# Third subtiles of at most 64 tokens in the experts' second product: 64-column fp32 matmuls in pairs instead of 24 split matmuls

## The chip, the cores and the metric

One core of a Trainium2 chip runs the whole program. The metric is the device time of one execution in microseconds (us), as the median of three runs. A profile of a further execution shows what each engine did: PE (TensorE, matmuls; PEld are its weight loads), DVE (VectorE), ACT (ScalarE), POOL (GpSimd) and SP (SyncE, which issues most of the DMAs).

## The reference

Three stages follow each other. Attention over keys and values that are pooled by 8, a mixture of experts, and a dense feed-forward layer:

```
attn = softmax(scale * q @ mean8(k).T) @ mean8(v)          # 8 x 8 heads, 576 tokens, 64 wide
x = tokens of attn                                          # 4608 x 512, fp32
skip tokens with x @ w_skip <= 0; e = argmax(x @ w_gate)    # 8 experts
h = relu(x[e] @ w1[e])                                      # 512 -> 1024
x[e] += gate * (h @ w2[e])                                  # 1024 -> 512
out = (silu(x @ w_in)) @ w_out                              # 512 -> 2048 -> 512
```

Which tokens go to which expert is known only when the program runs, and the change lies in the middle stage alone.

## The kernel before, in words

An expert's tokens are worked through in units of at most 384 tokens, three subtiles of 128. A list of units (`ut`) is made on the chip; one unit runs ahead of a loop, one behind it, and the loop `For_i` in `moe` takes the others, here 10. A unit has one of three widths by its number of tokens n: 384 (n over 320), 320 (n over 256) or 256. An expert with little more than 384 tokens is shared out so that its second unit has 256 tokens and up to 64 in the third subtile.

Each fp32 factor is split into a high part of the type fp32r and a low part that is the rest (`split`: ACT writes the high part, DVE the low one), and a product is made of three matmuls: high by high, low by high, high by low. In a unit:

- `mm1(n)` makes h for eight blocks f of 128 hidden columns. For each f, 12 matmuls of n columns go into one bank (tile `hp`, three banks in turn). Then ACT writes `hh[:, f]` and DVE `hl[:, f]`, and `conv2(raw2, f)` splits the raw w2 of the unit's expert, which lies in `raw2`, into `w2h` (ACT) and `w2l` (DVE).
- `second(e, cols, nxt, n, third)` first issues `load2(e)` (SP: raw w2 of the next unit's expert e into `raw2`, four DMAs, each of which waits until the two blocks it overwrites have been split). Then follow `xtrans((0, 1))` (transposes of the next unit's tokens on PE, split to `xth` and `xtl`), `gates()`, and `mm2(s, gt)` for the subtiles 2 and 1, each in a `tc.If(n > 128 s)`. Behind subtile 2 come its scatter (POOL) and `conv1(0..3)`, which splits the next expert's w1. At the end stand `xtrans((2, 3))` and `mm2(0, gt)`.
- `mm2(s, gt)` is 24 matmuls of 128 stationary columns by 512 (hh by w2h, hh by w2l, hl by w2h, for eight f) into tile `yp`, of which there are two banks, and one DVE instruction that scales by the gate and adds the tokens (`y`, shown as tile `x`).

All instructions of an engine run in the order in which they are written (class `Ordered`), and across the engines semaphores carry the waits. Nearly all rows bear the line L110, the helper that records them, so tiles tell them apart. `nc.before` and `nc.after` keep the instructions around an If in order on every engine.

Of the kernel before, what the change touches and what calls it, by code (L numbers as in the profile page):

```python
# [5 lines left out]
F32 = mybir.dt.float32  # L6
# [6 lines left out]
AF = mybir.ActivationFunctionType  # L13
ALU = mybir.AluOpType
# [4 lines left out]
P = 128  # L19
B, H, S, D = 8, 8, 576, 64  # L20
G = 72
NT = B * S
DM = H * D
# [129 lines left out]
class Kern:  # L153
# [638 lines left out]
    def moe(self, xa, up):  # L792
        nc, tc, c = self.nc, self.tc, self.c
        with tc.tile_pool(name="ms", bufs=1) as s1, \
             tc.tile_pool(name="mw", bufs=2) as s2, \
             tc.tile_pool(name="mp", bufs=2, space=PSUM) as pp:
            raw2, xn, xth, xtl, gi, si = self.raw2, self.xn, self.xth, self.xtl, self.gi, self.si
            hh = s1.tile([P, 8, U * P], F32R, name="hh", tag="hh")
            hl = s1.tile([P, 8, U * P], F32R, name="hl", tag="hl")
            xr = s1.tile([P, U, XW], F32, name="xr", tag="xr")  # L800
            y = self.x4[:, 0:U]

# [4 lines left out]
            def mm1(n, fs=range(8), conv=True):  # L807
                for f in fs:
                    ps = self.hp.tile([P, DM], F32, name=f"hp{f}_{n}", tag="hp")
                    i = 0  # L810
                    for w, x in ((self.w1h, xth), (self.w1h, xtl), (self.w1l, xth)):
                        for k in range(4):
                            nc.tensor.matmul(ps[:, 0:n], w[:, k, P * f:P * (f + 1)], x[:, k, 0:n],
                                             start=(i == 0), stop=(i == 11))
                            i += 1
                    self.split(hh[:, f, 0:n], hl[:, f, 0:n], ps[:, 0:n], relu=True)
                    if conv:
                        self.conv2(raw2, f)
                    else:
                        nc.scalar.copy(self.w2h[:, f], raw2[:, f])  # L820

            def scatter(s, other=None, si=si):

                ids = self.s2 if s == 2 and si is self.si else si[:, s:s + 1]
                ins = nc.gpsimd.indirect_dma_start(xa, bass.IndirectOffsetOnAxis(ap=ids, axis=0), y[:, s],
                                                   None, bounds_check=NT - 1, oob_is_err=False)
                if other:
                    tc.declare_no_dep(ins.ins, other.ins, reason="disjoint rows")
                return ins

            def gates():
                L = xr[:, :, DM:XW]
                v = nc.vector
                mx = s2.tile([P, U], F32, name="gmx", tag="gmx")
                v.tensor_reduce(mx, L, AX.X, ALU.max)
                d = s2.tile([P, U, E], F32, name="gd", tag="gd")
                v.tensor_tensor(d, L, bc(mx, 2, E), ALU.subtract)
                nc.scalar.activation(d, d, AF.Exp)
                gt = s2.tile([P, U], F32, name="gt", tag="gt")
                v.tensor_reduce(gt, d, AX.X, ALU.add)  # L840
                v.tensor_scalar(gt, gt, 1e-9, None, ALU.add)
                v.reciprocal(gt, gt)
                return gt

            def mm2(s, gt, between=None):
                ps = (pp if s else self.hp).tile([P, DM], F32, name=f"yp{s}", tag="yp" if s else "hp")
                i = 0
                for f in range(8):
                    if between and f == 4:
                        between()  # L850
                    for h, w in ((hh, self.w2h), (hh, self.w2l), (hl, self.w2h)):
                        nc.tensor.matmul(ps, h[:, f, P * s:P * (s + 1)], w[:, f], start=(i == 0), stop=(i == 23))
                        i += 1
                nc.vector.scalar_tensor_tensor(y[:, s, 0:DM], ps, gt[:, s:s + 1], xr[:, s, 0:DM], ALU.mult, ALU.add)

            load2 = lambda e: self.load_w2(e, raw2)
            for _ in self.slow:
                pass
            while len(self.todo) > 2:
                self.step()  # L860
            self.step()
            mm1(U * P, (0, 1), False)
            self.cpool = pp, "xt", 2, DM
            for f in range(3):
# [7 lines left out]
            for f, n in ((2, 5), (3, 7), (4, 7), (5, 7)):  # L872
                mm1(U * P, (f,), False)
                for _ in range(n):
                    next(units)
            self.read_table(nc.gpsimd)
            mm1(U * P, (6,), False)

            def low2(f):
# [9 lines left out]
            def second(e, cols, nxt, n=None, third=None):  # L889

                if n is not None:
                    load2(e)
                    self.xtrans((0, 1))
                gt = gates()
                self.rows(gi, nxt)
                nc.vector.tensor_scalar(self.s2, cols[:, U - 1:U] if third is None else third, -1.0, None, ALU.add)

                def convert(f):
                    for _ in self.ffn_ops(f):
                        pass  # L900
                    self.ffn_conv3(f)
                    self.ffn_load(f + 3)

                if n is None:
                    self.ffn_abs(0, self.raw1[:, 0], self.raw1[:, 1])
                    convert(0)
                for s in (2, 1):
                    if n is None:
                        mm2(s, gt)
                    else:  # L910
                        with tc.If(n > P * s) as cmp:
                            nc.before(cmp)
                            mm2(s, gt)
                        nc.after(cmp)
                    if s == 2:
                        scatter(s)
                        nc.vector.tensor_scalar(si[:, 0:U - 1], cols[:, 0:U - 1], -1.0, None, ALU.add)
                        if n is not None:
                            self.conv1(0)
                            self.conv1(1)  # L920
                            self.conv1(2)
                            self.conv1(3)
                if n is None:
                    self.xtrans((0, 1))
                    mm2(0, gt, lambda: self.xtrans((2, 3)))
                else:
                    self.xtrans((2, 3))
                    mm2(0, gt)
# [6 lines left out]
            for f in range(4, 8):  # L935
                low2(f)
            next(units)
            second(None, self.table[:, SLOTS:EMPTY], entry(1, 1, EMPTY, dve))
            for s in (1, 0, 2):
                nc.scalar.copy(y[:, s, DM:XW], xr[:, U - 1, DM:XW])  # L940
# [3 lines left out]
            with tc.For_i(0, nu, 1, iteration_sync="reg_based") as u:  # L944
                ld = lambda i, o, hi: nc.value(self.ut[0:1, i, bass.ds(u + o, 1)], hi)
                e = ld(0, 1, E - 1)
                self.load_w1(e)
                keep()
                n = ld(2, 0, U * P)
                cols, third = [self.table[:, bass.ds(ld(i, 0, EMPTY), m)] for i, m in ((1, U - 1), (3, 1))]  # L950
                nxt = ld(1, 2, EMPTY)
                self.gather(gi)
                scatter(1)
                scatter(0)
                with tc.If(n > 320) as cmp:
                    mm1(384)
                with cmp.Else():
                    with tc.If(n > 256) as cmp2:
                        mm1(320)
                    with cmp2.Else():  # L960
                        mm1(256)
                nc.after(cmp)
                second(e, cols, nxt, n, third)
# [23 lines left out]
            gt = gates()  # L987
# [11 lines left out]
            for s in (2, 1):  # L999
# [3 lines left out]
                while done:  # L1003
                    f = done.pop(0)
# [6 lines left out]
            while done:  # L1011
                f = done.pop(0)
# [554 lines left out]
```

## Time and profile before

| | us |
|---|---|
| median of three runs | 1315.89 (1315.4 to 1318.23) |
| the profiled execution's own time | 1316.77 |
| its span, first to last instruction | 1315.0 |
| PE busy | 1263.7 (96%) |
| DVE, ACT, POOL busy | 853.5, 569.4, 358.6 |
| the loop's four units of width 320 | 32.1, 31.8, 32.5, 33.8 |

The last row is read from the trace between the first `mm1` matmul of a unit and that of the next one. The loop runs from about 214 to 502 us of the span. The granted TensorE clock is at full speed (0.997 in the mean).

### The profile page before, as it was taken

How to read it: one execution, taken by the hardware profiler on the slowest of the kernel's cores; microseconds unless marked ns; L12 is line 12 of the kernel's file. 1: busy time of each engine (PE TensorE's matmuls, PEld its weight loads, DVE VectorE, ACT ScalarE, POOL GpSimd, SP SyncE). 2: the span in 40 equal slices, each digit the busy share in tenths (PEclk: the TensorE clock that was granted, in tenths of full speed). 3: DMA queues.
4: the chain of work that ended last, by engine and by line, in shares of the span. 5: the costliest groups of instructions: out<-in, count | busy, mean ns of one | idle time of the engine just before them, and what ended most of it. 6: DMA issues, size and time to landing. Idle time of an engine off the chain costs nothing.

```text
span 1315.0 us, 20410 instructions
## 1 busy us (share of the span) xinstructions
PE 1263.7 (96%) x6501; PEld 1076.1 (82%) x6502; DVE 853.5 (65%) x1553; ACT 569.4 (43%) x1188; POOL 358.6 (27%) x312
## 2 busy tenths in 40 slices
PE   6899788999989999999999999999999999999998
PEld 5788677988978888878888888788888888888887
DVE  4777776667667677779743325565784657847565
ACT  4666633454445454344433334534353333533321
POOL 4477433222223230322457603101011010111100
PEclk9999999999999999999999999999999999999999
DMA  9988635656556552248845322634356352463532
GB/s 288 294 271 250 211 129 197 202 178 208 181 181 210 196 191 84 89 164 277 280 169 210 141 97 88 224 124 172 120 185 210 142 176 93 163 208 129 176 106 95
DMA packets 94106, 233.77 MB, mean 178 GB/s; under 512 B 15068, under 2 KB 26972, under 8 KB 90375
## 3 DMA queue, kind: packets, MB, share of 16 engines
q1 hardware_dynamic: 86735, 215.82, 49.3%
q0 software_dynamic: 7008, 16.80, 3.9%
q8 instruction: 42, 0.69, 0.2%
q14 instruction: 33, 0.27, 0.1%
q10 hardware_dynamic: 288, 0.20, 0.1%
HBM read 182.58 MB, written 52.89 MB: 179 GB/s over the span
## 4 chain that ended last, share of the span: by engine, by line
PE 57%; DVE 3%; ACT 1%; issue 1%; POOL 0%; DMA 0%; DVEq 0%; ACTq 0%; POOLq 0%
PE yb L110 20%; PE ps L110 17%; PE fh L110 9%; PE fop L110 9%; PE yp L110 1%; DVE fr L110 1%; DVE ft L110 1%; PE hp L110 1%; PE fxp L110 0%; DVE raw L110 0%; PE sx L110 0%; DVE fgl L110 0%; DVE fsg L110 0%; ACT g L110 0%; DMA out<-fo 0%
## 5 line engine op out<-in xcount | busy, mean ns | idle before, releaser
L110 PE MATMUL yb<-wout,g 128*128 128x512 f32 x1152 | 268.5, 391 | 0.8 <-ACT st L110 0.4
L110 PEld LDWEIGHTS yb<-wout,g 128*128 128x128 f32 x1152 | 215.0, 188 | 45.7 <-DMA wout<-wdo 0.8
L110 POOL TENSOR_TENSOR tm<-tm,tm 128x512 f32<-128x512 f32 x24 | 32.1, 1339 | 411.5 <-ACT tm L110 411.5
L110 DVE TENSOR_TENSOR yacc<-yb,yacc 128x512 f32<-128x512 f32 x168 | 116.1, 691 | 38.2 <-PE yb L110 31.1
L110 ACT COPY tm<-ps 128x512 f32<-128x512 f32 x72 | 42.4, 589 | 146.2 <-PE ps L110 144.4
L110 PE MATMUL yp<-w2h,hh 128*128 128x512 f32 x240 | 96.4, 402 | 1.7 <-ACT w2h L110 1.3
L110 PE MATMUL yp<-w2l,hh 128*128 128x512 f32 x240 | 94.3, 393 | 2.2 <-DVE w2l L110 2.2
L110 PE MATMUL yp<-w2h,hl 128*128 128x512 f32 x240 | 94.3, 393 | 0.0
L110 ACT CAST g<-sg 128x512 fp32r<-128x512 f32 x96 | 59.6, 621 | 76.7 <-DVE sg L110 76.7
L110 ACT ACTIVATE hh<-hp 128x256 fp32r<-128x256 f32 (+2 forms) x96 | 41.2, 429 | 118.0 <-PE hp L110 107.0
L110 ACT ACTIVATE prb<-s,mx 128x72 f32<-128x72 f32 x288 | 65.4, 344 | 46.0 <-DVE mx L110 43.7
L110 DVE TENSOR_TENSOR fsg<-fh,fsg 128x512 f32<-128x512 f32 x48 | 33.0, 688 | 80.0 <-ACT fsg L110 80.0
L110 PE MATMUL fh<-w1l,fh 128*128 128x512 f32 x336 | 83.4, 390 | 0.0
L110 DVE TENSOR_TENSOR tm<-ps,tm 128x512 f32<-128x512 f32 x24 | 16.6, 690 | 98.1 <-PE ps L110 98.1
L110 PE MATMUL hp<-xth,w1h 128*128 128x256 f32 (+2 forms) x384 | 71.3, 307 | 5.3 <-issue 2.5
L110 PE MATMUL hp<-xtl,w1h 128*128 128x256 f32 (+2 forms) x384 | 72.2, 306 | 2.3 <-DVE xtl L110 1.9
L110 PEld LDWEIGHTS fh<-w1l,fh 128*128 128x128 f32 x336 | 62.8, 188 | 12.9
L110 DVE SCALAR_TENSOR_TENSOR hl<-hp,hh 128x256 fp32r<-128x256 f32 (+2 forms) x96 | 46.0, 479 | 40.5 <-ACT hh L110 36.6
L110 PE MATMUL hp<-xth,w1l 128*128 128x256 f32 (+2 forms) x384 | 69.9, 304 | 0.0
L110 DVE TENSOR_TENSOR g<-sg,g 128x512 fp32r<-128x512 f32 x96 | 65.7, 686 | 5.5 <-ACT g L110 5.1
L110 DVE TENSOR_TENSOR w2l<-raw,w2h 128x512 fp32r<-128x512 f32 x96 | 65.9, 691 | 3.3
L110 PE MATMUL pv<-vex,pts 120*128 120x148 f32 (+3 forms) x400 | 61.8, 308 | 4.9 <-remote 2.5
(230 smaller groups left out, 2750.2 us busy)
## 6 DMA issues: line engine op xcount, KB each, us to landing
raw<-w SPq DMA_DIRECT2D x88, 512.0 KB, 3.8
wout<-wdo SPq DMA_DIRECT2D x48, 512.0 KB
win<-wdi SPq DMA_DIRECT2D x36, 512.0 KB
w1l<-wdi SPq DMA_DIRECT2D x36, 512.0 KB
xa<-x SPq DMA_DIRECT2D x36, 256.0 KB
fx<-xa SPq DMA_DIRECT2D x9, 1024.0 KB
v<-vR SPq DMA_DIRECT2D x7, 1200.0 KB
fr<-w_in SPq DMA_DIRECT2D x16, 512.0 KB
```

The costliest lines, as they stand in the source:

```text
L110: ins = f(*a, **k)
```

## The change

In a unit of width 320 the third subtile's 64 tokens are no longer split. `mm1` splits the first 256 columns as before, and ACT writes the relu of the last 64 columns as plain fp32 into a new tile `hx`. In `second` the branch for subtile 2 gets a further `tc.If(n > 320)`: a unit with more tokens does `mm2(2)`, the others a new `mm2_half`. This makes eight fp32 matmuls with `hx[:, f]` as 64 stationary columns and the raw w2 block `raw2[:, f]` as 512 moving columns. Even f write the rows 0 to 63 of one bank, odd f the rows 64 to 127. ACT copies the upper half out, DVE adds the lower half to it, and a second DVE instruction scales by the gate and adds the tokens. As `mm2_half` reads `raw2`, the issue of `load2(e)` is moved from the start of `second` to behind the branch for subtile 2, in all units.

```diff
@@ -797,6 +797,7 @@
+            hx = s1.tile([P, 8, D], F32, name="hx", tag="hx")
...
-                    self.split(hh[:, f, 0:n], hl[:, f, 0:n], ps[:, 0:n], relu=True)
+                    if n == 2 * P + D:
+                        self.split(hh[:, f, 0:2 * P], hl[:, f, 0:2 * P], ps[:, 0:2 * P], relu=True)
+                        nc.scalar.activation(hx[:, f], ps[:, 2 * P:n], AF.Relu)
+                    else:
+                        self.split(hh[:, f, 0:n], hl[:, f, 0:n], ps[:, 0:n], relu=True)
...
+            def mm2_half(gt):
+                ps = pp.tile([P, DM], F32, name="yq", tag="yp")
+                for f in range(8):
+                    o = D * (f % 2)
+                    nc.tensor.matmul(ps[o:o + D], hx[:, f], raw2[:, f], start=(f < 2), stop=(f >= 6),
+                                     skip_group_check=True)
+                o = y[0:D, 2, 0:DM]
+                nc.scalar.copy(o, ps[D:P])
+                nc.vector.tensor_tensor(o, ps[0:D], o, ALU.add)
+                nc.vector.scalar_tensor_tensor(o, o, gt[0:D, 2:3], xr[0:D, 2, 0:DM], ALU.mult, ALU.add)
...
             def second(e, cols, nxt, n=None, third=None):
 
                 if n is not None:
-                    load2(e)
                     self.xtrans((0, 1))
...
                         with tc.If(n > P * s) as cmp:
                             nc.before(cmp)
-                            mm2(s, gt)
+                            if s == 2:
+                                with tc.If(n > 2 * P + D) as cmp2:
+                                    mm2(s, gt)
+                                with cmp2.Else():
+                                    mm2_half(gt)
+                            else:
+                                mm2(s, gt)
                         nc.after(cmp)
+                        if s == 2:
+                            load2(e)
```

The change moves instructions on ACT, PE and SP. On ACT, in `mm1` of width 320, this stood for the blocks f = 0 to 2 (the bracket names the engine or DMA queue whose semaphore is waited for; `raw_80` is `raw2`):

```order
L110 ACTIVATE hh<-hp_320_2934 128x320 [waits PE_I-2728_own,Activation_I-2728_own]
L110 REGISTER_ALU
L110 CAST w2h<-raw_80 128x512 [waits DMAHW4_I-2728_own,Activation_I-2728_own]
L110 ISA
L110 ACTIVATE hh<-hp_320_2951 128x320 [waits PE_I-2728_own,Activation_I-2728_own]
L110 REGISTER_ALU
L110 CAST w2h<-raw_80 128x512 [waits Activation_I-2728_own]
```

and now stands, for f = 0 and 1:

```order
L110 ACTIVATE hh<-hp_320_2935 128x256 [waits PE_I-2729_own,Activation_I-2729_own]
L110 REGISTER_ALU
L110 ACTIVATE hx<-hp_320_2935 128x64 [waits DVE_I-2729_own]
L110 REGISTER_ALU
L110 CAST w2h<-raw_80 128x512 [waits DMAHW4_I-2729_own,Activation_I-2729_own]
L110 ISA
L110 ACTIVATE hh<-hp_320_2953 128x256 [waits PE_I-2729_own,Activation_I-2729_own]
L110 REGISTER_ALU
L110 ACTIVATE hx<-hp_320_2953 128x64 [waits DVE_I-2729_own]
```

Between `hh` and `w2h` of each block ACT has a third instruction, and that one waits for DVE: it reads the same bank as DVE's `hl` of the block, and stands behind it.

On PE, the else branch of the inner If holds the eight matmuls of `mm2_half`; here are those for f = 0 to 3:

```order
L110 MATMUL yq<-raw_80,hx 64x512 [waits Activation_I-2729_own,DMAHW4_I-2729_own,DMAHW2_49]
L110 REGISTER_ALU
L110 MATMUL yq<-raw_80,hx 64x512 [waits Activation_I-2729_own]
L110 REGISTER_ALU
L110 MATMUL yq<-raw_80,hx 64x512 [waits DMAHW5_I-2729_own,Activation_I-2729_own,DMAHW3_49]
L110 REGISTER_ALU
L110 MATMUL yq<-raw_80,hx 64x512 [waits Activation_I-2729_own]
```

Lower and upper rows alternate, and every matmul waits for ACT's `hx` of its own block.

On SP, around the branch for subtile 2, `load2` stood ahead of it:

```order
L110 DMA raw_80<-w 128x2x512 [waits DMAHW4_I-2728_own,DVE_I-2728_own]
L110 ISA
L110 DMA raw_80<-w 128x2x512 [waits DMAHW5_I-2728_own,DVE_I-2728_own]
L110 ISA
L110 DMA raw_80<-w 128x2x512 [waits DMAHW6_I-2728_own,DVE_I-2728_own]
L110 ISA
L110 DMA raw_80<-w 128x2x512 [waits DMAHW7_I-2728_own,DVE_I-2728_own]
L911 COMPARE_AND_BRANCH
```

and now stands behind it:

```order
L926 COMPARE_AND_BRANCH [waits DVE_49]
L929 COMPARE_AND_BRANCH
L929 UNCONDITIONAL_BRANCH x2
L926 UNCONDITIONAL_BRANCH
L110 ISA
L110 DMA raw_80<-w 128x2x512 [waits DVE_I-2729_own,DMAHW4_I-2729_own,PE_I-2729_own,Activation_I-2729_own]
L110 ISA
L110 DMA raw_80<-w 128x2x512 [waits DVE_I-2729_own,DMAHW5_I-2729_own,PE_I-2729_own,Activation_I-2729_own]
```

The four DMAs of w2 now wait for PE as well, and no longer start one by one while `mm1` runs.

## Rows read from the trace of the kernel before

**Rows 1.** Page, part 1: busy time of PE, its share, instructions.
```profile
PE 1263.7 (96%) x6501; PEld 1076.1 (82%) x6502; DVE 853.5 (65%) x1553; ACT 569.4 (43%) x1188; POOL 358.6 (27%) x312
```
**Rows 2.** Stretch of one unit: length, busy by engine, clock, DMA share, GB/s.
```profile
332.40:364.19 31.79, 31.79 (x181) 28.86 (x180) 20.20 (x36) 13.94 (x26) 6.74 (x6) 1.00 0.53 177
```
**Rows 3.** Groups by form, 250 to 520 us: count, busy us, mean ns, idle before.
```profile
L110 PE MATMUL hp<-xth,w1h 128*128 128x320 f32 x128 | 24.0, 309 | 0.0
...
L110 ACT ACTIVATE hh<-hp 128x320 fp32r<-128x320 f32 x32 | 14.0, 438 | 44.9 <-PE hp L110 42.5 <-PE xtp L110 2.4
L110 DVE SCALAR_TENSOR_TENSOR hl<-hp,hh 128x256 fp32r<-128x256 f32 x32 | 13.6, 424 | 7.9 <-ACT hh L110 5.7 <-issue 1.2 <-ACT w2h L110 0.6
L110 ACT ACTIVATE hh<-hp 128x256 fp32r<-128x256 f32 x32 | 12.3, 385 | 35.9 <-PE hp L110 34.4 <-PE xtp L110 1.5
```
**Rows 4.** Timeline of PE in this unit: start, us, operation, count.
```profile
332.40 0.75 PE L110 MATMUL hp<-xth,w1h 128*128 128x320 f32 x4
...
346.48 0.82 PE L110 MATMUL xtp<-ident,xn 128*128 128x128 f32 x6
347.05 0.47 PE L110 MATMUL yp<-w2h,hh 128*128 128x512 f32 x1
...
358.07 0.82 PE L110 MATMUL xtp<-ident,xn 128*128 128x128 f32 x6
...
364.19 0.64 PE L110 MATMUL hp<-xth,w1h 128*128 128x256 f32 x4
```
**Rows 5.** Timeline of PE in attention: fp32 scores, 64 and 128 stationary columns.
```profile
44.37 1.25 PE L110 MATMUL s<-kbd,q 128*64 128x144 f32 x16
...
47.55 1.14 PE L110 MATMUL s<-kbd,q 128*128 128x144 f32 x8
```
**Rows 6.** The scores by tile: duration of one record, least, median, most (ns).
```profile
L110 PE MATMUL s<-kbd,q x320: 283/286/609, 9.4 to 158.9; 128*128 128x144 f32 x128, 128*64 128x144 f32 x32
```
**Rows 7.** Timeline of PE in attention: probabilities by values, 64 stationary columns.
```profile
55.75 2.54 PE L110 MATMUL pv<-vex,pts 120*64 120x148 f32 x20
```
**Rows 8.** Timeline of the weight loads there: idle before, in brackets.
```profile
55.75 2.27 PEld L110 LDWEIGHTS pv<-vex,pts 120*64 120x64 f32 x20 [0.17 <-PE pt L110]
58.22 0.54 PEld L110 LDWEIGHTS s<-kbd,q 128*128 128x128 f32 x4 [0.20 <-PE pv L110]
```
**Rows 9.** Timeline of ACT in the unit of rows 2.
```profile
346.76 0.44 ACT L110 ACTIVATE hh<-hp 128x320 fp32r<-128x320 f32 x1 [0.81 <-PE xtp L110]
347.10 0.61 ACT L110 CAST w2h<-raw 128x512 fp32r<-128x512 f32 x1
...
351.00 0.22 ACT L110 ACTIVATE gd<-gd 128x24 f32<-128x24 f32 x1 [2.54 <-DVE gd L110]
```
**Rows 10.** Timeline of DVE in the unit of rows 2.
```profile
347.23 0.49 DVE L110 SCALAR_TENSOR_TENSOR hl<-hp,hh 128x320 fp32r<-128x320 f32 x1 [0.56 <-ACT hh L110]
347.74 0.69 DVE L110 TENSOR_TENSOR w2l<-raw,w2h 128x512 fp32r<-128x512 f32 x1
...
350.73 0.18 DVE L110 TENSOR_TENSOR gd<-xr,gmx 128x24 f32<-128x24 f32 x1
...
352.12 0.15 DVE L110 TENSOR_SCALAR sq<-table 128x1 int32 x1
...
353.49 0.16 DVE L110 TENSOR_SCALAR si<-table 128x2 int32 x1
353.55 4.62 DVE L110 TENSOR_TENSOR w1l<-raw,w1h 128x1024 fp32r<-128x1024 f32 x4
...
359.19 1.02 DVE L110 TENSOR_TENSOR xtl<-xtp,xth 128x384 fp32r<-128x384 f32 x2 [0.17 <-ACT xth L110]
```
**Rows 11.** Page, part 5: evictions of a whole bank by ACT and DVE.
```profile
L110 ACT COPY tm<-ps 128x512 f32<-128x512 f32 x72 | 42.4, 589 | 146.2 <-PE ps L110 144.4
...
L110 DVE TENSOR_TENSOR tm<-ps,tm 128x512 f32<-128x512 f32 x24 | 16.6, 690 | 98.1 <-PE ps L110 98.1
```
**Rows 12.** A stretch in which raw w1 (2 MB) is loaded; columns of rows 2.
```profile
324.00:332.00 8.00, 8.00 (x40) 6.67 (x39) 4.16 (x6) 1.49 (x3) 0.00 (x0) 1.00 0.76 265
```

## The prediction

> **What bounds the kernel now.** I read the page first: PE is busy for 1263.7 of 1315.0 us [rows 1], so time is gained only where PE gets less to do, or waits less. The change lies in the loop over expert units, so next I cut the span into units by the first `mm1` matmul of each, and looked at the stretch from 332.40 to 364.19 us, a unit of width 320. PE is busy in all of its 31.79 us, at full granted clock, while DVE has 20.20 and ACT 13.94 us of work [rows 2]. Such a unit is bound by PE alone. How many units are touched follows from the form of `mm1`'s matmuls: 128 records of 320 columns in the group of xth and w1h [rows 3], 32 in a unit (8 blocks f by 4), so four units. The timeline of PE gives their course: `mm1` from 332.40 to 346.48, that is 14.08 us or 1.76 us for each f; six transposes; then `mm2(2)` and `mm2(1)` from 347.05 to 358.07, that is 11.02 us or 5.51 us for one `mm2`; the next unit begins at 364.19 [rows 4].
>
> **What goes and what comes on PE.** In each of the four units `mm2(2)`, 5.51 us, goes. In its place stand eight fp32 matmuls of 64 stationary by 512 moving columns. The loop has none, so I look at attention, which has fp32 matmuls with 64 and 128 stationary columns that write lower and upper rows of one bank. Four score matmuls of 128 columns show as 8 records: one fp32 matmul is two records. They take 1.14 us, the last of them 0.286 by itself [rows 5, 6], so the step from record to record is (1.14 - 0.286) / 7 = 0.122 us for 144 moving columns, 0.847 ns for a column. At 512 columns a record costs 0.434 us, and the 16 records of `mm2_half` cost 6.94 us one after the other, 3.47 us if lower and upper rows run side by side.
>
> They do in the scores: eight matmuls of 64 columns, four for the lower and four for the upper rows, are 16 records in 1.25 us [rows 5]. One after the other they would take 15 x 0.122 + 0.286 = 2.12 us; eight steps of pairs take 7 x 0.122 + 0.286 = 1.14. They are paired throughout, though each group of four lower records stands ahead of its four upper ones. In the product with the values ten lower records stand ahead of ten upper ones, eight of each ten with 148 and two with 222 columns. One after the other that is 16 x 0.125 + 4 x 0.188 + 0.16 for the end of the last = 2.92 us; the row shows 2.54 [rows 7], so only three steps were shared. PE thus looks a few records ahead, not ten. In `mm2_half` lower and upper alternate by matmul, so the partner of a record is at most two records behind it. I take full pairing, 3.47 us.
>
> The change from 128 to 64 columns and back costs something too: at the two ends of the 64-column stretch the weight loads stood idle for 0.17 and 0.20 us, both times waiting for PE [rows 8]. I take both, 0.37 us. So `mm2_half` costs 3.84 us in place of 5.51, and PE saves 1.67 us in a unit. With no cost at the ends it would be 2.04, with twice that cost 1.30.
>
> **What comes on ACT and DVE in `mm1`.** Here the change adds a wait. Before, ACT's hh and w2h of a block follow each other and DVE's hl and w2l run beside them [rows 9, 10]. Now ACT's new `hx` waits for DVE's hl, w2h is queued behind it, and DVE's w2l waits for w2h. The round for one f, from hl to the next hl: hl of 256 columns 0.424 [rows 3]; the wake of ACT by DVE 0.09 (gd ends at 350.91 and ACT's gd begins at 351.00) [rows 9, 10]; hx of 64 columns 0.226, from 385 ns at 256 and 438 at 320 columns (0.83 ns a column) [rows 3], between 0.22 for 24 columns [rows 9] and 0.385; less 0.10, since w2h begins 0.10 before the instruction ahead of it ends (346.76 + 0.44 against 347.10) [rows 9]; w2h 0.61; 0.03 until w2l (347.71 to 347.74) [rows 9, 10]; w2l 0.69. That is 1.97 us, or 1.87 if DVE overlaps its instructions as ACT does. I take 1.90, above PE's 1.76. Over seven rounds hl falls behind by 7 x 0.14 = 1.0 us. The three banks of `hp` cover that for PE, as the lag never reaches one block. Behind hl, w2l now begins 1.28 instead of 0.51 us later. In all DVE leaves `mm1` about 1.7 us later. `mm2_half` itself does not wait for it: its last pair begins six steps after its start, at about 349.8, and the last hx ends 1.0 + 0.09 + 0.23 us after the time at which hl was done before, 347.72, so at about 349.0.
>
> **What comes at the end of the half product.** PE is done at 347.05 + 0.17 + 3.47 = 350.7. ACT's copy stands behind gd, which is 1.7 us late, so from about 352.9; the copy is a whole-bank eviction of 0.589 [rows 11]: 353.5. DVE's sq, at 352.12 before, ends at 354.0; the branch takes at most the 0.55 us between sq's end and the next DVE instruction at 352.82 (si at 353.49 follows that) [rows 10]: 354.5. Then the add, 0.69 [rows 11], and the scaling, costed alike: si begins at 355.9 instead of 353.49, 2.4 us late. Queued behind it are the four w1l (4.62 us), the scaling of subtile 1 and the two xtl, 1.02 us [rows 10]: they end at about 362.6 instead of 360.2. PE's next `mm1`, begun at 364.19 - 1.67 = 362.5, takes the last xtl after seven matmuls of 256 columns, 7 x (1.76 / 12) x 256 / 320 = 0.8 us, at 363.3. So of 4.8 us of cover 0.7 is left. I cost the delay at nothing, and the cover that hides it is `mm2(1)` and `mm2(0)` on PE. POOL's scatter of subtile 2 moves with DVE, and nobody on PE waits for it.
>
> **What moves on SP.** `load2` now begins when `mm2_half` ends, 350.7, and the DMAs of the next unit's w1 and the rest of SP's loop are queued behind it. 2 MB came in 8 us at 265 GB/s [rows 12], so raw w2 is there at about 359, and its first quarter at 353; the first split of it comes behind the next unit's first block, after 363.9. Hidden by 5 us. Units with fewer tokens issue `load2` right behind the transposes; there the same 8 us stand against `mm2(1)` and `mm2(0)`, or `mm2(0)` alone in a unit of up to 128 tokens, where the quarters are used one by one. Nothing there either. Without that cover each us of delay would be one on PE.
>
> **Sum.** 4 x 1.67 = 6.7 us. The profiled execution took 1316.77, 1.77 us more than its span, and would take 1310.1; it lies 0.88 above the median of the runs. Against the median, 1315.89 - 6.7 = 1309.2 us, my prediction. Its own range, from the two bounds of the switch (8.2 and 5.2 us): 1307.7 to 1310.7.
>
> **Rivals.**
>
> *The round of ACT and DVE binds.* The round is put together from wakes and overlaps of other places. At 2.10 us the lag grows by 1.4 us more, 0.7 us beyond the cover; PE waits in the next `mm1` of three units (the fourth is followed by the end of the loop): 2.1 us lost, 1311.3. At 2.24 those three units gain nothing and 1314.2 is left; above it the change loses there. For it speaks that four engine changes now stand in a row; against it that each wake in the rows is 0.03 to 0.09 us. Chance 0.14.
>
> *The pairs do not form* (the slower side). Each matmul of `mm2_half` has a wait of its own and a register instruction ahead of it, those in the scores only the first. If PE took in one matmul at a time, `mm2_half` would cost 6.94 + 0.37 = 7.31 us, 1.80 more than `mm2(2)`: 4 x 1.80 = 7.2 us slower, 1323.1. It decides from where fewer than 1.80 / 0.434 = 4.1 of the eight steps are shared. Against it: the waits are for hx that is long there, but for the last. Chance 0.07.
>
> *Records start strictly in order.* Then each odd block starts a step after its even one: nine steps, 3.91 + 0.37 = 4.28 us, 1.23 us saved in a unit, 1311.0. The scores speak against it: in that order only 3 of 16 records would share a step, 12 x 0.122 + 0.286 = 1.75 us, and the row shows 1.25 [rows 5]. The Trainium skill, "TensorE: Matmul & The Clock Gate", section "Part 3: Packing small matmuls", states just this, that matmuls keep program order in start and end; the trace disagrees. Chance 0.05.
>
> *Weight loads lie open.* If the loads of a 64-column pair could not run beside its predecessor, each of eight steps would be longer by some 0.19 us, as at the ends [rows 8]: 1.5 us, 0.15 us saved, 1315.3. Against it: the 20 loads lie within the 2.54 us of their 20 records [rows 7, 8], which the steps fill. The same section of the Trainium skill states that a load overlaps running matmuls only with a different row group, which 128-row operands never have; the trace disagrees here too. Chance 0.03.
>
> **How the numbers follow.** Likeliest case 0.66, the rivals 0.14, 0.07, 0.05 and 0.03, and 0.05 for what the rows do not show (code fetched for the longer loop, the jumps of the inner If). A measurement can tell about 0.2%, 2.6 us. Faster by more: 0.66, 0.05 and 0.11 of the first rival, 0.82. Within it: the last rival, 0.02 of the first, 0.03 of the rest, 0.08. Slower: 0.07, 0.01 and 0.02, 0.10. The range 1307.5 to 1314.0 holds the likeliest case, the strict order and the first rival short of its break-even.
>
> **What would show it.** Four stretches of `yq` of 16 records in pairs, about 3.5 us; `hx` of 0.22 us starting 0.09 us behind hl; DVE's w2l at steps of 1.9 us; no wait of PE for xtl in the units that follow; raw w2 landed before its first split. A `yq` stretch of 5.5 us or more, or PE waiting for xtl or for `hp` behind hx by 2 us in a unit, would make the prediction wrong.

## The result, and the profile after

The changed kernel takes 1330.8 us (median of four runs, 1327.8 to 1334.0) against 1315.66 us (four runs): ratio 1.011, 95% interval 1.0096 to 1.0123. It is 15 us slower; forecast were 1309.2 us, from 1307.5 to 1314.0. The profiled execution of after was its shortest, 1327.8 us with a span of 1326.0, that is 11.0 above the span before.

PE has as much busy time as before (1263.7) in a span that is longer [rows 1]. From part 1 of the page:

```profile
PE 1263.8 (95%) x6469; PEld 1070.0 (81%) x6470; DVE 850.9 (64%) x1557; ACT 575.0 (43%) x1224; POOL 354.9 (27%) x312
```

I cut both traces at the first `mm1` matmul of each unit (u0 to u9 in the loop) and at the first matmul of the dense layer. Four stretches of before (length, busy time by engine, granted clock, DMA share, GB/s): u5 with u6, u9 with the loop's end, the unit behind the loop, the dense layer.

```profile
364.19:412.96 48.77, 43.99 (x289) 39.61 (x288) 35.17 (x67) 26.49 (x52) 14.46 (x12) 0.97 0.58 188
469.70:503.49 33.79, 32.20 (x182) 28.72 (x180) 21.86 (x40) 13.31 (x25) 7.58 (x6) 1.00 0.43 145
503.49:539.76 36.27, 35.62 (x184) 31.94 (x185) 29.83 (x42) 18.73 (x30) 10.65 (x6) 1.00 0.36 117
539.76:1315.00 775.24, 769.65 (x3457) 635.48 (x3455) 477.15 (x641) 296.01 (x467) 170.21 (x122) 1.00 0.47 161
```

The same of after, with u4 ahead, which answers to rows 2:

```profile
335.45:365.59 30.14, 30.14 (x174) 25.44 (x173) 19.53 (x37) 15.57 (x35) 7.07 (x6) 1.00 0.56 190
365.59:418.17 52.58, 45.20 (x290) 41.25 (x289) 36.98 (x69) 26.57 (x52) 14.51 (x12) 0.94 0.61 200
472.56:510.67 38.11, 30.75 (x173) 25.32 (x172) 24.24 (x44) 14.84 (x34) 6.84 (x6) 0.98 0.44 147
510.67:548.25 37.58, 37.58 (x184) 34.47 (x185) 30.07 (x42) 18.72 (x30) 10.50 (x6) 0.93 0.33 113
548.25:1326.00 777.75, 770.48 (x3457) 635.26 (x3455) 476.00 (x641) 295.98 (x467) 168.96 (x122) 1.00 0.46 160
```

That PE has no less busy time lies in part in stretches with a lower clock: 45.20 against 43.99 us in u5 and u6, 37.58 against 35.62 behind the loop.

Unit u4 has become 1.65 us shorter (31.79 to 30.14): the gain is real. It is lost elsewhere: u5 and u6 +3.81, u9 with the loop's end +4.32, the unit behind it +1.31, the dense layer +2.51; u3 +1.20 (33.34 against 32.14), u7 -2.35, the start up to the end of u2 +1.85, u8 nothing. The sum is 11.0.

Who made PE wait? The waits of PE in the loop (us, times, longest), before:

```profile
PE hp L110 <- PEq L1563: 1.5, 1, 1.5
PE hp L110 <- DVE xtl L110: 1.3, 2, 1.2
```

and after:

```profile
PE hp L110 <- DVE xtl L110: 9.6, 3, 4.3
PE hp L110 <- PEq L1586: 4.6, 1, 4.6
```

The three waits for `xtl` stand at the head of `mm1` in u3, u6 and u9, and each follows a unit of up to 256 tokens, which has no `mm2_half` at all. The other line is the loop's end.

**The chain in u2.** SP's four DMAs of raw w2 (start of the first, time from it to the end of the last, count), before:

```profile
280.74 8.87 SPq L110 DMA_DIRECT2D raw<-w  x4
```

and after:

```profile
290.14 2.49 SPq L110 DMA_DIRECT2D raw<-w  x4
```

The first waits until PE is past the branch; by then all of `raw2` is free, and the four that were spread over `mm1` go out in one burst. POOL's scatter of subtile 0 is issued into it. The timeline of POOL after (in brackets idle time and releaser):

```profile
288.69 1.02 POOL L110 DMA_INDIRECT xa<-x,si  x1 [3.90 <-DMA xn<-xa,gi]
292.39 1.00 POOL L110 DMA_INDIRECT xa<-x,si  x1 [2.69 <-DMA xa<-x,si]
300.40 1.57 POOL L110 DMA_INDIRECT xa<-x,sq  x1 [7.00 <-DVE si L110]
```

From issue to landing the second of these took 7.2 us, in before 2.8 (its view by tile, before and then after):

```profile
DMA to landing us min/median/max: 2.8/2.8/2.8
```
```profile
DMA to landing us min/median/max: 7.2/7.2/7.2
```

In the first 3.6 us behind it the 16 DMA engines were busy at 0.97; in before, in the 2.84 us until its landing, at 0.42 (columns as above; before, then after):

```profile
292.11:294.95 2.84, 2.84 (x17) 2.43 (x16) 0.88 (x5) 2.63 (x4) 1.01 (x1) 1.00 0.42 161
```
```profile
292.39:296.00 3.61, 3.61 (x18) 2.93 (x17) 1.94 (x9) 1.94 (x3) 1.00 (x1) 1.00 0.97 267
```

DVE rewrites `si`, which that scatter reads, and so waits for the landing with everything queued behind it. DVE after:

```profile
294.81 0.15 DVE L110 TENSOR_SCALAR sq<-table 128x1 int32 x1
299.70 0.17 DVE L110 TENSOR_SCALAR si<-table 128x2 int32 x1 [4.74 <-DMA xa<-x,si]
299.89 4.63 DVE L110 TENSOR_TENSOR w1l<-raw,w1h 128x1024 fp32r<-128x1024 f32 x4
304.44 0.74 DVE L110 SCALAR_TENSOR_TENSOR x<-yp,gt,xr 128x512 f32<-128x512 f32 x1
305.10 1.01 DVE L110 TENSOR_TENSOR xtl<-xtp,xth 128x384 fp32r<-128x384 f32 x2
```

and PE, which began u3 at 302.11:

```profile
305.79 0.85 PE L110 MATMUL hp<-xtl,w1h 128*128 128x320 f32 x2 [2.64 <-DVE xtl L110]
```

DVE was idle for the last 4.74 of the 7.2 us in which the scatter landed, and in before it was busy in 2.63 of the 2.84; so it was not DVE's work that held POOL's DMA up.

**The loop's end.** POOL's instructions there, by line (count, ns least/median/most, first and last start), before and then after:

```profile
L1563 POOLq DRAIN  x2: 119/4878/9636, 492.2 to 503.0; - x2
```
```profile
L1586 POOLq DRAIN  x2: 119/4880/9642, 500.4 to 510.2; - x2
```

Behind its last scatter POOL drains for 9.64 us, and every engine waits for that. Before, the drain began at 492.2, ended at 501.9 and was hidden behind PE and DVE. After, it begins at 500.4 and ends at 510.0, while PE's last matmul ends at 506.1: PE stands still until 510.67, for 4.6 us instead of 1.5. The granted clock behind it (columns as above):

```profile
506.00:508.00 2.00, 0.09 (x1) 0.00 (x0) 0.75 (x1) 0.00 (x0) 0.00 (x0) 1.00 0.00 0
512.00:514.00 2.00, 2.00 (x7) 2.00 (x7) 1.93 (x3) 0.43 (x1) 0.79 (x1) 0.50 0.33 127
516.00:518.00 2.00, 2.00 (x12) 2.00 (x11) 1.47 (x3) 0.31 (x1) 1.25 (x1) 0.92 0.15 48
```

From 510 to 516 us PE ran at 0.50, the lower of its two levels (1.2 GHz); before, with 1.5 us of idle time, it stayed at 1.00.

### The profile page after: what moved, and what is told of

The parts are those of the page before. It is cut to its first block, busy times and chain, and to the rows that moved or that the text cites. A ratio compares the mean times of both kernels' runs of the same rounds, so it can differ in the third digit from the quotient of the medians.

```text
span 1326.0 us, 20468 instructions
## 1 busy us (share of the span) xinstructions
PE 1263.8 (95%) x6469; PEld 1070.0 (81%) x6470; DVE 850.9 (64%) x1557; ACT 575.0 (43%) x1224; POOL 354.9 (27%) x312
## 4 chain that ended last, share of the span: by engine, by line
PE 58%; DVE 1%; issue 1%; DMA 0%; ACT 0%; SPq 0%; DVEq 0%
PE yb L110 20%; PE ps L110 17%; PE fop L110 9%; PE fh L110 9%; PE hp L110 1%; PE yp L110 1%; PE fxp L110 0%; DMA wout<-wdo 0%; DVE ft L110 0%; DVE fr L110 0%; PE sx L110 0%; DVE fgl L110 0%; DVE fsg L110 0%; SPq L110 0%; DVE sg L110 0%
## 5 line engine op out<-in xcount | busy, mean ns | idle before, releaser
L110 PE MATMUL yp<-w2h,hh 128*128 128x512 f32 x208 | 84.5, 406 | 1.8 <-ACT w2h L110 1.8
L110 ACT ACTIVATE hh<-hp 128x256 fp32r<-128x256 f32 (+1 forms) x96 | 39.3, 410 | 105.6 <-PE hp L110 100.0
L110 PE MATMUL yp<-w2l,hh 128*128 128x512 f32 x208 | 82.1, 395 | 2.3 <-DVE w2l L110 2.3
L110 PE MATMUL yp<-w2h,hl 128*128 128x512 f32 x208 | 82.1, 395 | 0.0
L110 PEld LDWEIGHTS hp<-xtl,w1h 128*128 128x128 f32 x384 | 61.4, 195 | 12.4 <-issue 11.1
```

The source lines that it names most:

```text
L110: ins = f(*a, **k)
```

## The experiments

Theory A was the chain above: burst, landing, `si`, `w1l`, `xtl`, `mm1`. Rival B was my main rival from the prediction, the new round of ACT and DVE (with `mm2_half` and its evictions). Ratios are to the kernel before on the same chip, with the 95% interval. "Stalls" are PE's waits for `xtl` at the head of `mm1` in the loop.

**e1_move_only**, the kernel before with one edit:

```diff
-                    load2(e)
                     self.xtrans((0, 1))
...
+                        if s == 2:
+                            load2(e)
```

> Kernel before, with one part of the change alone: the load of raw w2 (four DMAs, 2 MB) stands behind the branch of subtile 2; no mm2_half, no hx. Theory A (the moved load collides with the scatter of subtile 0; its landing holds DVE's si and POOL's next scatter, and behind si the four w1l, xtl and the next mm1): PE stalls of 2 to 5 us at the head of three mm1 that follow units of up to 256 tokens, 10.5 us in all, and some at the loop's end: 1324 to 1330 us. Rival B (the round of ACT and DVE with hx, or mm2_half and its evictions, hold DVE back): the load alone costs nothing, 1315 to 1317 us.

1.0004 (0.9994 to 1.0014): no change, and my number was a miss. The trace shows why: the four DMAs still took 8.87 us from first to last. Without `mm2_half` nobody on PE reads `raw2`, so SP runs past the branch ahead of the others. Where the load stands in the program doesn't matter here; what it waits for does.

**e5_burst_alone** is e1 with that wait put in, and nothing else:

```diff
                     self.xtrans((0, 1))
+                    hold = pp.tile([P, DM], F32, name="hold", tag="yp")
+                    nc.tensor.matmul(hold[:, 0:8], raw2[:, 0, 0:P], raw2[:, 0, 0:8], start=True, stop=True)
```

> Kernel before with the load behind the branch, and one small fp32 matmul per unit (8 moving columns, result unused) that reads raw2 behind the first transposes, so that SP can't issue the load of raw w2 until PE is there: four DMAs in a burst, as in after, without mm2_half and hx. The matmul itself costs up to 0.2 us a unit, 2 us in all. Theory A (the burst of 2 MB holds up the scatter of subtile 0, and behind its landing stand si, w1l, xtl and mm1): stalls of 2 to 5 us at the head of three mm1 behind units of up to 256 tokens, and POOL's last scatter later, so 2 to 4 us more at the loop's end: 1326 to 1332 us. Rival B (the stalls need hx or mm2_half): 1316 to 1319 us.

1332.95 us, 1.0125 (1.0106 to 1.0144), without `hx` and `mm2_half`. That this is as much as after is chance: after also saves 6.6 us on PE and loses 6.9 at the loop's end, in the unit behind it and in the dense layer. The load and the scatter of e5 in u2, and its waits:

```profile
288.19 2.26 SPq L110 DMA_DIRECT2D raw<-w  x4
```
```profile
DMA to landing us min/median/max: 7.8/7.8/7.8
```
```profile
PE hp L110 <- DVE xtl L110: 10.0, 3, 4.5
PE hp L110 <- PEq L1566: 1.5, 1, 1.5
```

Theory A holds for the three stalls, and rival B falls: they come without `hx` and `mm2_half`, and u3, u5 with u6, and u9 with the loop's end are 4.7, 4.5 and 4.6 us longer than in before, 13.8 of the 14.1 us by which the span is longer. Only the loop's end was not longer, against my number: here PE has the full `mm2(2)` and is as late as POOL.

**e2_si_late**, after with the write of `si` behind `mm2(0, gt)`, the last eviction of the unit:

> Kernel after, with one DVE instruction moved: the write of si stands behind the last eviction of the unit, so that w1l and xtl are not queued behind its wait for the landing of the scatter. Theory A: the three stalls (2.9, 4.6, 3.0 us in the profile) go, POOL's wait for the same landing stays and with it the 3 us at the loop's end: 1319 to 1322 us. If instead the load held back raw w1 or PE's own operands, nothing changes: 1329 to 1332 us.

1.003 (1.0013 to 1.0047), 1319.09 us. The waits for `xtl` at the head of `mm1` are gone, and the median's distance from before falls from 15.1 to 3.1 us; the loop's end now waits for 8.5 us (see the last section).

**e3_early_small**, after with `load2` at the head of the stage where `n` is at most 256, else behind the inner branch:

> Kernel after, but units of up to 256 tokens, which do not read raw w2, issue its load at the head of the stage as before; the others behind the branch. Theory A: the scatter of subtile 0 lands within about 3.5 us again in those units, the three stalls go: 1318 to 1322 us, with the loop's end still 3 us longer. Rival B (hx round, mm2_half): 1329 to 1332 us.

0.999 (0.9978 to 1.0002), 1314.47 us, better than expected, but not shown to be faster than before. In u2 the load is spread over 8.85 us again and the three stalls shrink to about 0.6 us; the loop's end stays at 5.2 us.

**e4_half_alone**, after with the load at its old place; `mm2_half` reads `self.w2h[:, f].bitcast(F32)` instead of `raw2[:, f]`:

> Kernel after with the load at its old place in all units; so that raw w2 may be overwritten, mm2_half multiplies by w2h (the high part alone, read as fp32; the low part of w2 is left out for these 64 rows). This is mm2_half, hx and the inner branch without the move. Theory A: 4 times 1.9 us saved on PE, less 3 us at the loop's end (POOL's drain of 9.6 us begins with the last scatter, which DVE releases later): 1310 to 1313 us. Rival B: no better than after, 1328 to 1332 us.

1.0012 (0.9997 to 1.0027), 1316.3 us: neither theory's number. The loop is 3.6 us shorter, but the unit behind it takes 37.37 instead of 36.27 us and the dense layer 2.3 us more. So this build gains nothing even without the burst. The 2.3 us come with a wait of DVE of 2.50 us ahead of `ft`, the one that e15 looks into below.

**e6_no_third**, e3 without the loop's `scatter(2)`:

> Kernel after with the early load in units of up to 256 tokens, and without the scatter of subtile 2 in the loop (left out: the rows of the third subtile are not written back). Theory on the loop's end (POOL's drain takes 9.6 us from its last scatter, and all engines wait for it): the last scatter is now that of subtile 0, some 10 us earlier, the drain is hidden, PE's gap falls from 5.6 to 1.9 us and the low clock behind it goes: 1309 to 1311 us. Rival C (the gap is DVE's or SP's tail, or fetched code): 1314 to 1315 us.

0.9954 (0.9939 to 0.9968), 1311.0 us. u9 with the loop's end takes 32.45 us, against 36.22 in e3, and no clock falls behind it: POOL's drain sets the loop's end.

**e7_early_hx**, e3 with ACT's `hx` ahead of `self.split(hh, hl)`; **e8_early_hx_gates**, in addition `gates()` and the writes of `gi` and `sq` ahead of `xtrans((0, 1))` (the expectations in this order):

> Kernel after with the early load in units of up to 256 tokens, and ACT's hx ahead of hh and DVE's hl, so that ACT waits for DVE no more. DVE should leave mm1 1.8 us earlier in the four units, the last scatter 1.8 us earlier, and the loop's end with it: 1311.5 to 1313 us. If the round of ACT and DVE has no part in the loop's end: 1314 to 1315 us.

> As the kernel with early load and hx first, and the gates (and the two index writes) stand ahead of the first transposes' splits, in DVE's idle 1.6 us there: the last scatter another 1.5 us earlier, the drain nearly hidden, and si earlier in each unit: 1309 to 1311.5 us. If the gap at the loop's end does not hang on the last scatter: as the other, within 1 us.

e7: 0.9971 (0.9957 to 0.9986), 1313.11 us; the wait at the loop's end falls from 5.2 to 3.6 us, as expected. e8: 0.9967 (0.9954 to 0.9981); the last scatter came only 0.5 us earlier behind `mm2_half`, not 1.5, and the ratio can't be told from that of e7.

**e9 to e12**: the scatter of subtile 2 is held back to the head of the next unit, to get it away from the loop's end. e9 is e7 with that alone, e10 also has the late `si`; e11 and e12 have both on before and on after.

```diff
                 scatter(1)
                 scatter(0)
+                scatter(2)
...
                     if s == 2:
-                        scatter(s)
```

> As the kernel with early load and hx first, and the scatter of subtile 2 is held back to the head of the next unit, behind those of subtiles 1 and 0 (one more behind the loop). POOL's last DMA in the loop then lies some 15 us ahead of its end. Theory on the drain: the gap at the loop's end falls to 1.9 us and the low clock behind it goes, 3 us better than that kernel: 0.994 of before, about 1309 us. If the drain doesn't decide: 0.997, as without the deferral.

> As the kernel with early load, hx first and the deferred scatter, and the write of si behind the last eviction of the unit. The stalls of 0.4 to 2 us that are left at the head of mm1 go (w1l and xtl no longer behind the landing): 0.992 to 0.994 of before, 1306 to 1309 us. If a late si delays the scatters at the head of the next unit and these something on PE: no better or worse than without it.

> Control: kernel before with the deferred scatter and the late write of si alone. Before has 1.3 to 2.6 us of waits for the landing in PE's path and a drain that is hidden by 1 us: 0.998 to 1.000 of before. If it gains as much as in the changed kernel, the gain there is not a repair of the change: 0.994.

> Kernel after with the deferred scatter and the late write of si, the load in a burst behind the branch as in after. Theory A: the burst still delays the landing of the scatter to 7 us, but nothing on PE's path hangs on it any more: 0.994 to 0.996 of before, 1309 to 1312 us. If the burst costs by itself (raw w2 or w1 late, or the scatters at the head late): 1315 us or more.

All missed by far: e9 1.0163 (1.0138 to 1.0188), e10 1.0136 (1.0114 to 1.0159), e11 1.0176 (1.0156 to 1.0197), e12 1.0273 (1.0253 to 1.0292). I had walked into the same trap with the other index. DVE in u2 of e9:

```profile
306.93 0.15 DVE L110 TENSOR_SCALAR sq<-table 128x1 int32 x1 [5.32 <-DMA xa<-x,sq]
```

DVE's write of `sq` now waits for the third landing of a chain of three, with `w1l` and `xtl` behind it; the control e11 shows that it needs nothing of the change. What the burst costs when nothing on PE's path hangs on the scatter, the question of e12, stays open.

**e13_second_defer** mends that: e7, with `scatter(2)` first at the head of the next unit, and both index writes last; **e16_before_defer2** is that deferral on the kernel before, **e14_early_hx_si** is e7 with only `si` late (the expectations in this order).

```diff
+                scatter(2)
                 scatter(1)
                 scatter(0)
...
                     mm2(0, gt)
+                    nc.vector.tensor_scalar(self.s2, third, -1.0, None, ALU.add)
+                    nc.vector.tensor_scalar(si[:, 0:U - 1], cols[:, 0:U - 1], -1.0, None, ALU.add)
```

> As the kernel with early load and hx first; the scatter of subtile 2 is held back to the head of the next unit, now ahead of those of subtiles 1 and 0, and both index writes (sq and si) stand behind the last eviction, so that DVE waits for no landing ahead of w1l and xtl. Theory (the deferral lost 18 us only because DVE's write of sq waited for the third landing with xtl behind it; and POOL's drain sets the loop's end): gap at the loop's end 1.9 us, no low clock behind it, no stall at the head of mm1: 0.993 to 0.995 of before, 1307 to 1310 us. If the deferral costs by itself: over 1320 us.

> Control: kernel before with that deferral (scatter of subtile 2 first at the head of the next unit, index writes last) alone. Before has 1.0 us of slack in POOL's drain and short waits for the landing only: 0.998 to 1.000 of before. If it gains as much as in the changed kernel, 0.994 or less, the gain is not the repair of the change.

> As the kernel with early load and hx first, with the write of si behind the last eviction; scatters as in after. The stalls left at the head of mm1 (0.4 to 1.4 us, 2.3 in all in the profile) go, the loop's end stays 3.6 us: 0.995 to 0.997 of before, 1310 to 1312 us. If si was not what held xtl: 0.997, as without.

e13: 1309.96 us, 0.997 (0.9945 to 0.9995); its runs spread from 1304.9 to 1324.4, so only "faster than before" is shown, not a gain over e7. As with e7 and e8, the interval lies below 1, and far below that of after. POOL's drain and PE's wait at the loop's end:

```profile
L1595 POOLq DRAIN  x2: 113/4468/8822, 485.7 to 496.4; - x2
```
```profile
PE hp L110 <- PEq L1595: 1.7, 1, 1.7
```

The drain begins early enough to be hidden, with no work left out. But "no stall" was a miss: u8 takes 29.76 us, in e7 24.26, and the loop, 286.99 us, is no shorter than that of e7, 286.80. POOL and DVE in u7:

```profile
427.61 5.02 POOL L110 DMA_INDIRECT xa<-x,si  x1 [5.33 <-DMA xa<-x,si]
```
```profile
438.65 0.75 DVE L110 SCALAR_TENSOR_TENSOR x<-yp,gt,xr 128x512 f32<-128x512 f32 x1 [5.29 <-DMA xa<-x,si]
```

This scatter is slow, and DVE's last scaling overwrites what it reads; behind it in DVE's order stand `sq`, `si` and the first `hl` of u8, and PE waits for DVE there. e16: 1.002 (1.0009 to 1.0031), so the deferral by itself gains nothing; in the changed kernel it mends the loop's end. e14: 0.9997 (0.9987 to 1.0008), a miss: the stalls went, but the wait at the loop's end grew to 6.8 us (see the last section).

**e15_after_pad**: where do the 2.5 us in the dense layer come from? DVE in its first block, after:

```profile
555.22 0.69 DVE L110 TENSOR_SCALAR ft<-fr 128x1024 uint32<-128x1024 uint32 x1 [2.73 <-issue]
```

It idles for nothing that is waited for, and in the view of the DMAs from 552 to 556 us stand two packets of code:

```profile
q14 instruction: 2, 0.02, 1.2%
```

The edit puts 32 small memsets of DVE behind the loop under `tc.If(nu > NU - 3)`, which is not taken.

> Kernel after with 32 small DVE instructions behind the loop in a branch that is not taken, so that DVE's later code lies elsewhere. In after and two more kernels DVE idles 2.5 to 2.7 us ahead of ft in the first dense block for nothing that is waited for, and the dense layer is 2.5 us longer; a fetch of code lies at that time. Theory (the place of a fetch in DVE's code): that wait goes or moves, from fh to the end 771.2 us again instead of 773.8, 1328 us. If the wait comes from the late loop end or from data: 773.8 and 1331 us.

1326.43 us, 1.0081 (1.0065 to 1.0097), against 1.011 for after. The wait is gone and the dense layer is back at 775.2 us (the expectation counts it from a matmul 4 us further on):

```profile
554.13 0.68 DVE L110 TENSOR_SCALAR ft<-fr 128x1024 uint32<-128x1024 uint32 x1
```

So these 2.5 us hang on where DVE's code lies. That the fetch itself is the cause is not shown: in before two packets of code stand at the same place, from 543 to 548 us, and DVE does not wait there.

## Why the prediction was wrong

**The product on PE: right.** `mm2_half` saves 1.65 us in u4, forecast were 1.67. The pairs form: in the trace the two records of a pair start 7 ns apart, and the pairs follow at steps of 0.43 us. PE after (compare [rows 4]):

```profile
349.53 0.82 PE L110 MATMUL xtp<-ident,xn 128*128 128x128 f32 x6
350.27 3.65 PE L110 MATMUL yq<-raw,hx 128*64 128x512 f32 x16
353.86 0.50 PE L110 MATMUL yp<-w2h,hh 128*128 128x512 f32 x1
```

All four stretches show it, so the rivals on pairs, strict order and open weight loads are out.

**The round of ACT and DVE in `mm1`: right.** DVE and then ACT in u4, against [rows 9, 10]:

```profile
348.95 0.42 DVE L110 SCALAR_TENSOR_TENSOR hl<-hp,hh 128x256 fp32r<-128x256 f32 x1
350.22 0.69 DVE L110 TENSOR_TENSOR w2l<-raw,w2h 128x512 fp32r<-128x512 f32 x1 [0.84 <-ACT w2h L110]
350.82 0.42 DVE L110 SCALAR_TENSOR_TENSOR hl<-hp,hh 128x256 fp32r<-128x256 f32 x1
...
358.55 0.15 DVE L110 TENSOR_SCALAR si<-table 128x2 int32 x1
```
```profile
349.41 0.22 ACT L110 ACTIVATE hx<-hp 128x64 f32<-128x64 f32 x1 [0.81 <-DVE hl L110]
```

The round is 1.87 us (forecast 1.90), and `si` stands 23.1 us behind the unit's start (forecast 355.9 - 332.4 = 23.5). In the units behind a unit of width 320 PE does not wait for `xtl`, as I said; so this rival did not decide. At the loop's end, where the prediction did not look for it, the round takes part: with `hx` ahead of it (e7) PE waits 1.6 us less there.

**What moves on SP: the step that failed.** "Nothing there either" was said of the units with fewer tokens. I had the burst and its 8 us about right (in u2 of e15 the four land within 9.4 us of the first issue), and asked only whether raw w2 would be there in time. I did not ask what else needed the DMA engines in those 8 us, nor who waits for that: the scatter, and on DVE `si`, `w1l` and `xtl`. The price is 9.6 us of waits in three units, and u6 then runs in part at the lower clock (0.94 over u5 and u6, before 0.97). My answer to "what would make it wrong", PE waiting for `xtl` by 2 us in a unit, is what came, but for another reason.

**"Nobody on PE waits for it": wrong at one place.** I had POOL's last scatter 2.4 us later and PE 1.67 us earlier, and never followed the loop's end. Before, the drain ended at 501.9 and DVE's last step at 502.7; with my own two numbers it is late by 2.4 + 1.67 - 0.9 = 3.2 us. Measured are 3.04, and 1.3 for the lower clock behind them.

**The rest**: 2.5 us in the dense layer; I had 0.05 for "what the rows do not show" and named fetched code there, with no size. Open are 1.85 us between the start and the end of u2; 1.37 of them lie ahead of the loop, where profiles differ by more than that anyway: in the 18 kernels, whose code is the same up to the first unit, that unit begins between 169.7 and 175.4 us. In the median after stands 4 us further from before than in the profiles; no trace shows those.

## What to carry to other kernels

When a load gets a new reader, look at what it waits for now and what else uses the DMA engines from there on: a spread load that becomes a burst is paid by small scatters, and then by whoever rewrites their indices. Ahead of every in-order wait, list what is queued behind it; an index write belongs behind the work that needs no index, but e13 and e14 show that the wait can come up again at another place. A loop's end is a place of its own: find which engine drains last there before saying that a delay off the critical path is free.

## What the runs showed of the hardware

The drain at the loop's end took 9.64 us behind an indirect DMA of 1.30 us in before, after, e3, e4 and e7. In e14 the last scatter itself took 4.63 us and the drain 12.99:

```profile
485.66 4.63 POOL L110 DMA_INDIRECT xa<-x,sq  x1 [7.86 <-DVE x L110]
```

It did so in the four units of width 320 of e2 and e14, where DVE's four `w1l` follow the eviction at once; with `si` between them, as in e7, it took 1.30 beside the same four `w1l`. The 5.02 us in u7 of e13 stand beside four `w1l` too. The Trainium skill, "SBUF — State Buffer", section "SBUF: two separate sides", says that a DVE instruction with two inputs in SBUF and a GpSimd instruction that reads SBUF lock each other out of a shared pair of ports: whichever starts first holds it for its whole length. The 4.63 us would fit that, if `w1l` and the scatter are such instructions, which no run shows; the 1.30 us in e7 would not. The cause stays open.
